# Zero products ahead of the first head mix, and the first batch's v loaded by pairs of heads, twice

## The chip, the cores and the metric

The kernel runs on one core of a Trainium2 chip. The metric is the device time of one launch in microseconds; three runs give a median of 743.95 (743.8 to 744.45). Engines are called by the names of the profile: PE (matrix products), PEld (its weight loads), DVE (vector), ACT (scalar), POOL (GpSimd) and SP, whose queue issues every DMA of this kernel.

## The reference, cut to what matters

```python
scores = scale * np.matmul(q, k.transpose(0, 1, 3, 2))      # 2 batches, 12 heads, 448 rows, head size 64
scores = np.einsum('bhij,hg->bgij', scores, w_pre)          # first mix, over heads
scores = scores - np.max(scores, axis=-1, keepdims=True)
attn = np.exp(scores)
attn = attn / (np.sum(attn, axis=-1, keepdims=True) + 1e-09)
attn = np.einsum('bhij,hg->bgij', attn, w_post)             # second mix
x = np.matmul(attn, v)                                      # then as 896 x 768
# two feed-forward layers, 768 -> 2048 -> 768, first with ELU, then with SiLU
```

## The kernel before

The kernel computes attention first (to about 270 us of the trace) and the two layers after it. Attention works on eight tiles: batch 0 or 1, times four groups of up to 120 query rows. The scores of a tile lie in SBUF as rows by heads (`s`). A mix over heads needs heads on the partitions, so a DMA (`relayout`) brings ten query rows by twelve heads into a block of 120 partitions by 448 keys (`blk`, five buffers). There are twelve blocks in a full tile and nine in the fourth one, 90 in all.

An order written out by hand runs over the blocks: one call of `step(s)` issues the work of step s for each engine. In step s PE mixes block s (`premix`, `pre`), DVE takes the row maximum (`rmax`, `nmx`), ACT takes exp with the row sum (`exps`), and DVE makes the reciprocal of the sum for block s-1 (`recip`: `sum`, `kr`). PE makes the second mix of block s-2 (`postmix`, `post`), and ACT and DVE split the result of block s-3 into two fp16 parts (`post_hi`, `post_lo`, tile `a`). Other work hangs on the steps in tables: `QK_AT` (score products of the next tile, `pq`, and transposes of q, `ptq`), `KT_AT` (transposes of the second batch's k), `X_AT` (products with v, `av`), `P_AT` and `V_AT` (work on v), and `D_AT` (DMAs). Each engine runs its instructions in the order in which they are issued, and SP its DMAs too: a DMA that waits holds all behind it.

v is used as two fp16 parts after a scaling by a power of two, so its largest magnitude must be known first. `v_max` takes the maximum of two heads at a time (DVE), and `v_scale` brings the six results to one scale in three stages: a DVE reduction, a PE transpose with a DVE reduction (`vpa`, `vmb`), and a PE broadcast (`vpb`) followed by six small DVE instructions. `prep_v` makes the parts of a pair: two ACT instructions, and the remainders either on DVE (even pairs of batch 0, `v_lo` in the next step) or on POOL (`vf`, then a subtraction).

For batch 0, all of v comes in step 0 by three DMAs of 448 KB (`vraw`), ahead of the relayout of block 5. The maxima stand in steps 1 to 6, the scale in 7 to 9, the parts in 9 to 12. The first products with v stand in step 15, two heads in every second step from then on. Batch 1's v comes by pairs (`vr`, two buffers, 224 KB each): the loads for the maxima in steps 16 to 26, the maxima in 18 to 28, the scale in 30 to 32, and a second load for the parts from step 39 on.

Ahead of step 0 the first tile is built under a PSUM pool of its own. PE runs 14 products on zeros, then transposes of q and k, then six pairs of score products. A pair's two heads fill one PSUM tile of two banks, from which ACT takes the first head and DVE the second. Relayouts 0 to 4 follow, then the transposes of the second tile's q, and then step 0.

Of the kernel before, what the change touches and what calls it, by code (L numbers as in the profile page):

```python
# [8 lines left out]
F32 = mybir.dt.float32  # L9
# [4 lines left out]
AF = mybir.ActivationFunctionType  # L14
ALU = mybir.AluOpType
AX = mybir.AxisListType
PSUM = bass.MemoryType.PSUM

P = 128
B, H, S, D = 2, 12, 448, 64  # L20
# [3 lines left out]
NP = H // 2  # L24
CP = S // 4
# [6 lines left out]
NBLK = 5  # L32
PREB = 3
NWARM = 14
NE = 3
LAG = (2, 3)

# [2 lines left out]
def attn_moe_moe(ctx: ExitStack, tc: tile.TileContext, q, k, v, w_pre, w_post, w1i, w1o, w2i, w2o, out):  # L40
    nc = tc.nc
# [9 lines left out]
    cm_b, bp = pool("attn1", bufs=1, side="right")  # L51
    cm_a, ap_ = pool("attn2", bufs=1, side="left")
    cm_p0, p0 = pool("ps0", bufs=1, space=PSUM)
    psp = [p0]
# [100 lines left out]
    def transpose_q(T, g):  # L155
        m = prows(tiles[T][1])
        raw = raws["q", T]
        pt = ps.tile([P, S], F32, name=f"ptq{T}_{g}", tag="pre", bufs=PREB) if T else p0.tile([P, S], F32, name=f"ptq{T}_{g}", tag="t", bufs=3)
        pt = pt[:, :3 * TI]
        pt = pt.rearrange("p (j c) -> p j c", j=3)  # L160
        for j in range(3):
            p = 3 * g + j
            nc.tensor.transpose(pt[:, j, :m], raw[:m, 2 * p:2 * p + 2].rearrange("p e d -> p (e d)"), ident[:m, :m])
        if g == 0:
            qT[T] = wp.tile([P, 2, NP, P], F32R, name=f"qt{T}", tag="qT", bufs=3)
        t = qT[T][:, :, 3 * g:3 * g + 3, :m]

        o = [t[:, i].rearrange("p j (r n) -> p j r n", r=BI) for i in range(2)]
        tev.append((o[0], o[1], pt[:, :, :m].rearrange("p j (n r) -> p j r n", r=BI)))

    def transpose_hi():

        for hi, lo, src in tev:
            nc.scalar.copy(hi, src)
# [10 lines left out]
    ones = cp.tile([1, P], F32, name="ones1")  # L185
    nc.vector.memset(ones, 1.0)

    def load_v0(g):
        if g == 0:
            vraw[0] = ap_.tile([CP, H, 4, D], F32, name="vraw0", tag="a", bufs=2)  # L190
        nc.sync.dma_start(vraw[0][:, 4 * g:4 * g + 4], v[0, 4 * g:4 * g + 4].rearrange("h (p r) d -> p h r d", r=4))

    def load_v1(p):
        raw = bp.tile([CP, 2, 4, D], F32, name=f"vr_{p}", tag="vr", bufs=2)
        nc.sync.dma_start(raw, v[1, 2 * p:2 * p + 2].rearrange("h (p r) d -> p h r d", r=4))
        vraw[1, p % NP] = raw

    def v_max(b, p):
        if p == 0:
            vmx[b] = cp.tile([CP, NP], F32, name=f"vmx{b}")  # L200
        raw = vraw[0][:, 2 * p:2 * p + 2] if b == 0 else vraw[1, p]
        nc.vector.tensor_reduce(vmx[b][:, p:p + 1], raw.rearrange("p h r d -> p (h r d)"), axis=AX.X, op=ALU.max, apply_absolute_value=True)

    vst = {}

# [30 lines left out]
    def prep_v(b, p):  # L236

        t = ap_.tile([CP, 4, 2, P], F16, name=f"v16_{b}_{p}", tag="v16", bufs=7)
        sc = vs[b][0][:CP]
        raw = vraw[0][:, 2 * p:2 * p + 2] if b == 0 else vraw[1, p]  # L240
        for e in range(2):
            hi = t[:, :, e, e * D:(e + 1) * D]
            nc.scalar.activation(hi, raw[:, e], AF.Copy, scale=sc)
            lo = t[:, :, e, (1 - e) * D:(2 - e) * D]
            if b or p % 2:
                full = ap_.tile([CP, 4, D], F32, name=f"vf{p}_{e}", tag="vf", bufs=2)
                nc.gpsimd.tensor_scalar(full, raw[:, e], sc, None, op0=ALU.mult)
                nc.gpsimd.tensor_tensor(lo, full, hi, op=ALU.subtract)
            else:
                vev.append((lo, raw[:, e], sc, hi))  # L250
        v16[b, p] = t
# [5 lines left out]
    def qk_pair(T, p):  # L257

        b, t = tiles[T]
        m = prows(t)  # L260
        if T not in smap:
            smap[T] = bp.tile([TI, H, S], F32, name=f"s{T}", tag="s", bufs=2)
        qt, kt = qT[T][:, :, p], kT[b, p]
        pq = psp[0].tile([P, 2, 512], F32, name=f"pq{T}_{p}", tag="mm", bufs=2 if T == 0 else 1)[:m, :, :S]
        for n, (i, j) in enumerate(((0, 0), (0, 1), (1, 0))):
            for e in range(2):
                half = slice(e * D, (e + 1) * D)
                nc.tensor.matmul(pq[:, e], qt[half, i, :m], kt[half, j, :], start=(n == 0), stop=(n == 2))  # L268
        sev.append((T, p, m, pq))

    def qk_evac():
        for T, p, m, pq in sev:
            o = smap[T][:m, 2 * p:2 * p + 2, :]
            if T == 0:
                nc.scalar.activation(o[:, 0], pq[:, 0], AF.Copy, scale=0.125)
                nc.vector.tensor_scalar(o[:, 1], pq[:, 1], 0.125, None, op0=ALU.mult)
            else:
                nc.scalar.activation(o, pq, AF.Copy, scale=0.125)
        sev.clear()
# [14 lines left out]
    def relayout(n):  # L294

        T, i0, ni = blocks[n]
        t = bp.tile([TI, S], F32, name=f"blk{n}", tag="blk", bufs=NBLK)
        k = nblk(tiles[T][1])
        i = i0 // BI
        dl[n] = nc.sync.dma_start(t[:ni * H], smap[T][i:i + k * (ni - 1) + 1:k])  # L300
        blk[n] = t
# [150 lines left out]
    cm_p0.__exit__(None, None, None)  # L452
    cm_ps, ps = pool("psA", bufs=1, space=PSUM)
    psp[0] = ps
    transpose_q(1, 0)
    transpose_q(1, 1)
    transpose_hi()
    transpose_lo()
    prep_mix()
# [2 lines left out]

    NB = len(blocks)
    NT_ = len(tiles)
    QK_AT, KT_AT, X_AT, P_AT, V_AT, D_AT = {}, {}, {}, {}, {}, {}

    def at(d, step, f):
        d.setdefault(int(step), []).append(f)

    for T in range(NT_):  # L470
        b, t = tiles[T]
        f, l = first[T], last[T]
        sc = (l - f + 1) / 12
        if T + 1 < NT_:
            nb, nt_ = tiles[T + 1]
            for p in range(NP):
                st = (max(2 * p - 2, p if p < 2 else 0) if T == 0 else int(f + (2 * p - 2) * sc + 8) - 8)
                at(QK_AT, st, lambda TT=T + 1, p=p: qk_pair(TT, p))
                if nt_ == 3 and nb + 1 < B:
                    at(KT_AT, st + 3, lambda p=p, bb=nb + 1: transpose_k(bb, p))  # L480
                    at(D_AT, st - 3 if p < 2 else st, lambda p=p, bb=nb + 1: load_k(bb, p))
            n0 = NBLK if T + 1 == 0 else 0
            for n in range(first[T + 1] + n0, last[T + 1] + 1):
                at(D_AT, max(l - 1, n - NBLK + 1), lambda n=n: relayout(n))
        if T + 2 < NT_:
            at(D_AT, 0 if T == 0 else f + 1, lambda TT=T + 2: load_q(TT))
            for g in range(2):
                at(QK_AT, l - 3 + 2 * g, lambda TT=T + 2, g=g: transpose_q(TT, g))
        for p in range(NP):
            if T + 1 < NT_:  # L490
                nsc = (last[T + 1] - l) / 12
                st = l + 1 + LAG[1] + (p if T + 2 == NT_ else int(2 * p * nsc))
            for h in (2 * p, 2 * p + 1) if T + 1 < NT_ else ():
                at(X_AT, st, lambda T=T, h=h: av_head(T, h))
            if t == 3 and b + 1 < B:
                v1 = [l - 1] + [l + 2 + LAG[1] + int(2 * j * nsc) for j in range(NP - 1)]
                at(V_AT, v1[p], lambda p=p, b=b: prep_v(b + 1, p))
                at(D_AT, l - 5 + p if p < 2 else v1[p - 2] + 2, lambda p=p: load_v1(p))
    for n in range(NBLK, last[0] + 1):
        at(D_AT, n - NBLK + 1, lambda n=n: relayout(n))  # L500
    for g in range(3):
        at(D_AT, 0, lambda g=g: load_v0(g))
    for p in range(NP):
        at(V_AT, 1 + p, lambda p=p: v_max(0, p))
        at(V_AT, 9 + 0.7 * p, lambda p=p: prep_v(0, p))
        at(D_AT, 16 + 2 * p, lambda p=p: load_v1(p))
        at(V_AT, 18 + 2 * p, lambda p=p: v_max(1, p))
    for b, st in ((0, 7), (1, 30)):
        for i in range(3):
            at(V_AT if i == 0 else P_AT, st + i, lambda b=b, i=i: v_scale(b, i))  # L510

    def run(d, s):
        for f in d.get(s, []):
            f()

    def step(s):
        def do(f, n):
            if 0 <= n < NB:
                f(n)

        do(premix, s)
        run(QK_AT, s)
        run(P_AT, s)
        do(post_hi, s - LAG[1])
        do(rmax, s)
        do(recip, s - 1)
        do(post_lo, s - LAG[1])
        v_lo()
        av_sum()
        av_swap()  # L530
        av_evac()
        run(X_AT, s)
        run(KT_AT, s)
        do(postmix, s - LAG[0])
        do(exps, s)
        transpose_hi()
        qk_evac()
        transpose_lo()
        run(V_AT, s)
        run(D_AT, s)  # L540


# [409 lines left out]
```

## Time and profile before

| | before |
|---|---|
| median of 3 runs | 743.95 us |
| the profiled execution: time / span | 746.99 us / 745.2 us |
| PE busy in the span | 722.4 us, 97% |
| DVE / ACT / POOL busy | 516.2 / 398.1 / 74.7 us |
| granted PE clock, mean | 0.991 |

A line of a timeline gives start, duration, engine, line of the kernel, operation, output and inputs, shapes and count, and in brackets how long the engine was idle before it and what ended that. A PE instruction on fp32 counts twice (x2 is one product of the first mix), and its end is modelled, so costs on PE are read from one start to the next.

### The profile page before, as it was taken

The page shows a single profiled execution, that of the slowest core. Times are in us where ns is not written, and L with a number is a line of the kernel's source. Part 1 is how long each engine was busy: PE and PEld are TensorE (multiplying, and loading weights), DVE is VectorE, ACT ScalarE, POOL GpSimd, SP SyncE. Part 2 cuts the span into 40 slices and gives each one's busy share as a digit, 9 for nine tenths or more (in the row PEclk, how much of TensorE's full clock was granted, in tenths as well). Part 3 has the DMA queues.
Part 4 walks back from the last instruction along what each step waited for, and adds up shares of the span by engine and source line. Part 5 has one row for each costly group of instructions (what it writes and reads, how often), then busy time and mean ns, then how long its engine had stood idle before and what let it go on. Part 6 is the DMA issues. An engine that isn't in the chain of part 4 may idle for free.

```text
span 745.2 us, 12122 instructions
## 1 busy us (share of the span) xinstructions
PE 722.4 (97%) x4472; PEld 616.4 (83%) x4472; DVE 516.2 (69%) x1147; ACT 398.1 (53%) x789; POOL 74.7 (10%) x99
## 2 busy tenths in 40 slices
PE   7889999999998899999999999999999999999998
PEld 4456766776775688999999999999999999999997
DVE  5687877677776868888885556567888888833800
ACT  5577767788775657666663223335555555312301
POOL 1033011355123320000000000000000000000000
PEclk9899999999999999999999999999999999999999
DMA  6724735344325233333333333342333334633402
GB/s 121 219 82 130 188 103 146 117 122 142 105 95 173 81 114 106 105 109 107 106 102 104 113 113 113 113 127 83 110 104 108 106 107 119 183 102 106 139 1 74
DMA packets 90435, 85.70 MB, mean 115 GB/s; under 512 B 32664, under 2 KB 86280, under 8 KB 90376
## 3 DMA queue, kind: packets, MB, share of 16 engines
q1 hardware_dynamic: 90376, 84.93, 39.0%
q8 instruction: 35, 0.57, 0.3%
q14 instruction: 24, 0.20, 0.1%
HBM read 60.05 MB, written 2.75 MB: 84 GB/s over the span
## 4 chain that ended last, share of the span: by engine, by line
PE 90%; DVE 5%; DMA 3%; SPq 1%; ACT 1%; issue 0%; ACTq 0%
PE ph L716 30%; PE po L769 16%; PE post L352 9%; PE pre L310 7%; PE py L791 5%; PE py L789 5%; PE py L790 5%; PE pq L268 4%; PE av L385 4%; PE ph_mm L716 1%; DVE a L366 1%; DVE nmx L318 1%; DMA vraw<-in_v_dram 1%; DMA xs<-xt 1%; DVE kr L341 1%; PE ptk L151 1%
## 5 line engine op out<-in xcount | busy, mean ns | idle before, releaser
L716 PE MATMUL ph<-x,we 128*128 128x448 f32 x1116 | 231.0, 369 | 2.5 <-ACT x L559 1.5
L716 PEld LDWEIGHTS ph<-x,we 128*128 128x128 f32 x1116 | 210.7, 189 | 22.2 <-ACT x L559 1.8
L352 PE MATMUL post<-kr,pe 120*112 120x120 f32 x720 | 93.8, 273 | 9.0 <-DVE a L366 8.5
L769 PE MATMUL po<-g,we 128*128 128x448 f32 x468 | 101.5, 366 | 0.0
L352 PEld LDWEIGHTS post<-kr,pe 120*112 120x112 f32 x720 | 80.5, 177 | 25.1 <-issue 17.7
L769 PEld LDWEIGHTS po<-g,we 128*128 128x128 f32 x468 | 87.8, 188 | 7.9
L328 ACT ACTIVATE pe<-pre,nmx 120x448 f32<-120x448 f32 x90 | 57.1, 634 | 62.9 <-DVE sum L338 54.2
L310 PE MATMUL pre<-blk,kpre 120*120 120x448 f32 x180 | 85.3, 556 | 2.4 <-DMA blk<-s 2.4
L318 DVE TENSOR_REDUCE nmx<-pre 120x1 f32<-120x448 f32 x90 | 55.9, 622 | 43.9 <-PE pre L310 43.6
L617 ACT ACTIVATE wr<-wr 128x384 f32<-128x384 f32 x126 | 67.3, 545 | 35.5 <-DMA wr<-in_moe_w_out_dram 31.2
L652 ACT CAST we<-wc 128x768 fp32r<-128x768 f32 (+1 forms) x63 | 51.0, 809 | 41.8 <-PE py L791 22.3
L659 DVE TENSOR_TENSOR we<-wc,we 128x768 fp32r<-128x768 f32 (+1 forms) x63 | 58.6, 930 | 19.5 <-ACT we L652 16.7
L632 DVE SCALAR_TENSOR_TENSOR wc<-wr,wc 128x384 int32<-128x384 int32 x126 | 68.8, 546 | 4.3
L634 DVE SCALAR_TENSOR_TENSOR wc<-wr,wc 128x384 int32<-128x384 int32 x126 | 68.5, 543 | 3.3
L366 DVE TENSOR_TENSOR a<-post,a 112x480 f16<-112x480 f32 x90 | 58.5, 650 | 5.2 <-ACT a L361 5.2
L790 PE MATMUL py<-we,g 128*128 128x384 f32 x182 | 61.0, 335 | 0.0
L791 PE MATMUL py<-we,g 128*128 128x384 f32 x182 | 61.0, 335 | 0.0
L789 PE MATMUL py<-we,g 128*128 128x384 f32 x182 | 61.0, 335 | 0.0
L385 PEld LDWEIGHTS <-v 112*128 112x128 f16 x768 | 42.2, 99 | 20.5 <-issue 18.3
L361 ACT ACTIVATE a<-post 112x480 f16<-112x480 f32 x90 | 51.6, 573 | 6.5 <-PE post L352 6.5
L385 PE MATMUL av<-a,v 112*128 112x120 f16 (+1 forms) x768 | 46.0, 215 | 0.9 <-DVE a L366 0.9
L268 PEld LDWEIGHTS pq<-kt,qt 64*120 64x120 f32 (+1 forms) x288 | 21.9, 175 | 29.2 <-ACT a L361 11.2
(111 smaller groups left out, 866.6 us busy)
## 6 DMA issues: line engine op xcount, KB each, us to landing
wr<-in_moe_w_in_dram SPq DMA_DIRECT2D x58, 384.0 KB
wr<-in_moe_w_out_dram SPq DMA_DIRECT2D x56, 384.0 KB
blk<-s SPq DMA_DIRECT2D x90, 210.0 KB
wr<-in_moe_w_out_dram SPq DMA_DIRECT2D x12, 256.0 KB
vr<-in_v_dram SPq DMA_DIRECT2D x12, 224.0 KB
out_dram<-y SPq DMA_DIRECT2D x14, 192.0 KB
early<-in_moe_w_in_dram SPq DMA_DIRECT2D x6, 384.0 KB
xs<-xt SPq DMA_DIRECT2D x36, 60.0 KB
```

Source lines behind the costliest of these rows:

```text
L310: nc.tensor.matmul(t[:r], kpre[:r].rearrange("p i h -> p (i h)")[:, :r], blk.pop(n)[:r], start=True, stop=True)
L352: nc.tensor.matmul(t[:CP, j, :, :ni], pp[:r, j * CP:(j + 1) * CP], k[:r, :, :ni], start=True, stop=True)
L366: nc.vector.tensor_tensor(a[:, 1, :, :, i0:i0 + ni], pst.pop(n)[:CP, :, :, :ni], a[:, 0, :, :, i0:i0 + ni], op=ALU.subtract)
L385: nc.tensor.matmul(o, vt[:, j, h % 2, :], a[:, c, j, h, :m], start=(c == 0 and j == 0), stop=(c == 1 and j == 3))
L617: nc.scalar.activation(hf, hf, AF.Copy, scale=2.0 ** -112)
L632: nc.vector.scalar_tensor_tensor(cc, r[:, :, 1], -2147483648, cc, op0=ALU.bitwise_and, op1=ALU.bitwise_or)
L634: nc.vector.scalar_tensor_tensor(cc, r[:, :, 0], 29, cc, op0=ALU.logical_shift_right, op1=ALU.bitwise_or)
L716: nc.tensor.matmul(ph, wt[:, kk * P:(kk + 1) * P], xq[hf, kk][:, xi], start=(n_ == 0), stop=(n_ + 1 == len(terms)))
L769: nc.tensor.matmul(po, wt[:, kk * P:(kk + 1) * P], g_out1(k0 + kk, gi, hf), start=(k0 == 0 and n_ == 0), stop=(k0 + kn == KF and n_ == 3 * ...
L789: nc.tensor.matmul(py, gh, hi[:, w_], start=(kf == 0), stop=False)
L790: nc.tensor.matmul(py, gh, lo[:, w_], start=False, stop=False)
L791: nc.tensor.matmul(py, gl, hi[:, w_], start=False, stop=(kf == KF - 1))
```

## The change

- Sixteen products on zeros are issued on PE ahead of step 0: seven before the transposes of the second tile's q and nine after them. They write a buffer of the `pre` ring that nothing reads.
- In the first tile, a pair's score products go to two PSUM tiles of one bank each, in place of one tile of two banks.
- v of batch 0 is loaded by pairs, as that of batch 1 is, through the same two buffers, and twice. The loads for the maxima stand in steps 0, 0, 2, 4, 6 and 8, those for the parts in steps 10, 12, ... 20. The maxima stand in steps 2, 4, 6, 8, 9 and 10, the scale in 10 to 12, and the parts in steps 13, 15, ... 23.
- Batch 1's first loads move to steps 24 to 34, its maxima to 26 to 36 and its scale to 38 to 40.
- The PE stages of the scale (`P_AT`) are issued after `exps` in a step, no longer right after the first mix.
- Relayouts have a table of their own (`R_AT`), issued ahead of a step's other DMAs.

```diff
+NKEEP = (7, 9)
...
-    def load_v0(g):
-        if g == 0:
-            vraw[0] = ap_.tile([CP, H, 4, D], F32, name="vraw0", tag="a", bufs=2)
-        nc.sync.dma_start(vraw[0][:, 4 * g:4 * g + 4], v[0, 4 * g:4 * g + 4].rearrange("h (p r) d -> p h r d", r=4))
-    def load_v1(p):
-        raw = bp.tile([CP, 2, 4, D], F32, name=f"vr_{p}", tag="vr", bufs=2)
-        nc.sync.dma_start(raw, v[1, 2 * p:2 * p + 2].rearrange("h (p r) d -> p h r d", r=4))
-        vraw[1, p % NP] = raw
+    def load_v(b, p):
+        raw = bp.tile([CP, 2, 4, D], F32, name=f"vr{b}_{p}", tag="vr", bufs=2)
+        nc.sync.dma_start(raw, v[b, 2 * p:2 * p + 2].rearrange("h (p r) d -> p h r d", r=4))
+        vraw[b, p] = raw
...
-        pq = psp[0].tile([P, 2, 512], F32, name=f"pq{T}_{p}", tag="mm", bufs=2 if T == 0 else 1)[:m, :, :S]
+        if T == 0:
+            pq = [p0.tile([P, S], F32, name=f"pq0_{p}_{e}", tag=f"mm{e}", bufs=2)[:m] for e in range(2)]
+        else:
+            pq = psp[0].tile([P, 2, 512], F32, name=f"pq{T}_{p}", tag="mm", bufs=1)[:m, :, :S]
...
+    def keep(i):
+        t = ps.tile([P, S], F32, name=f"keep{i}", tag="pre", bufs=PREB)
+        for _ in range(NKEEP[i]):
+            nc.tensor.matmul(t, wz[:, :P], wz, start=True, stop=True)
+
+    keep(0)
     transpose_q(1, 0)
     transpose_q(1, 1)
+    keep(1)
...
-                at(D_AT, max(l - 1, n - NBLK + 1), lambda n=n: relayout(n))
+                at(R_AT, max(l - 1, n - NBLK + 1), lambda n=n: relayout(n))
...
-        at(D_AT, n - NBLK + 1, lambda n=n: relayout(n))
-    for g in range(3):
-        at(D_AT, 0, lambda g=g: load_v0(g))
+        at(R_AT, n - NBLK + 1, lambda n=n: relayout(n))
     for p in range(NP):
-        at(V_AT, 1 + p, lambda p=p: v_max(0, p))
-        at(V_AT, 9 + 0.7 * p, lambda p=p: prep_v(0, p))
-        at(D_AT, 16 + 2 * p, lambda p=p: load_v1(p))
-        at(V_AT, 18 + 2 * p, lambda p=p: v_max(1, p))
-    for b, st in ((0, 7), (1, 30)):
+        at(D_AT, max(0, 2 * p - 2), lambda p=p: load_v(0, p))
+        at(V_AT, (2, 4, 6, 8, 9, 10)[p], lambda p=p: v_max(0, p))
+        at(D_AT, 10 + 2 * p, lambda p=p: load_v(0, p))
+        at(V_AT, 13 + 2 * p, lambda p=p: prep_v(0, p))
+        at(D_AT, 24 + 2 * p, lambda p=p: load_v(1, p))
+        at(V_AT, 26 + 2 * p, lambda p=p: v_max(1, p))
+    for b, st in ((0, 10), (1, 38)):
         for i in range(3):
             at(V_AT if i == 0 else P_AT, st + i, lambda b=b, i=i: v_scale(b, i))
...
         do(premix, s)
         run(QK_AT, s)
-        run(P_AT, s)
...
         do(exps, s)
+        run(P_AT, s)
         transpose_hi()
         qk_evac()
         transpose_lo()
         run(V_AT, s)
+        run(R_AT, s)
         run(D_AT, s)
```

## Rows read from the trace of the kernel before

**Rows 1.** Windows: stretch, length, busy time of each engine, PE clock, DMA share, GB/s.
```profile
18.20:19.87 1.67, 0.00 (x1) 0.04 (x1) 1.48 (x9) 0.00 (x0) 0.00 (x0) 0.52 0.58 220
19.87:25.00 5.13, 5.13 (x12) 1.91 (x14) 0.90 (x3) 1.64 (x3) 0.00 (x0) 0.50 0.86 222
...
60.43:108.00 47.57, 47.57 (x406) 33.98 (x405) 37.02 (x104) 33.53 (x73) 5.76 (x9) 1.00 0.61 165
```

**Rows 2.** Timeline of PE, from before step 0 to step 15.
```profile
16.69 0.81 PE L163 MATMUL ptq<-ident,q 120*128 120x120 f32 x6 [1.04 <-DMA q<-in_q_dram]
19.87 1.82 PE L310 MATMUL pre<-blk,kpre 120*120 120x448 f32 x2 [2.37 <-DMA blk<-s]
...
41.96 0.53 PE L163 MATMUL ptq<-ident,q 120*128 120x120 f32 x3
...
60.43 0.92 PE L310 MATMUL pre<-blk,kpre 120*120 120x448 f32 x2
```

**Rows 3.** The chain that ended last, 14 to 32 us: start, length, what.
```profile
15.70 0.55 ACT s L275
...
16.27 0.64 DVE s L276
...
16.93 0.85 SPq L300
...
21.68 6.72 DMA vraw<-in_v_dram
```

**Rows 4.** Waits from 19.8 to 60.43 us: total, times, longest.
```profile
PE post L352 <- DVE a L366: 3.6, 6, 1.6
```

**Rows 5.** Timeline of DVE in steps 6 and 7.
```profile
37.52 0.61 DVE L318 TENSOR_REDUCE nmx<-pre 120x1 f32<-120x448 f32 x1
...
39.78 0.61 DVE L318 TENSOR_REDUCE nmx<-pre 120x1 f32<-120x448 f32 x1
...
41.46 0.15 DVE L210 TENSOR_REDUCE vma<-vmx 112x1 f32<-112x6 f32 x1
```

**Rows 6.** Instructions of line 276: what ended its engine's idle time (us, times).
```profile
  ACT s L275: 1.5, 6
```

**Rows 7.** Timeline of PE's weight loads for zero products at the start.
```profile
4.66 0.29 PEld L434 LDWEIGHTS <-wz 128*128 128x128 f16 x2 [0.20 <-issue]
4.85 0.29 PEld L434 LDWEIGHTS <-wz 128*128 128x128 f16 x2
```

**Rows 8.** Timeline of PE in steps without a wait.
```profile
62.89 0.92 PE L310 MATMUL pre<-blk,kpre 120*120 120x448 f32 x2
...
64.54 1.07 PE L352 MATMUL post<-kr,pe 120*112 120x120 f32 x8
65.45 0.92 PE L310 MATMUL pre<-blk,kpre 120*120 120x448 f32 x2
...
123.85 0.92 PE L310 MATMUL pre<-blk,kpre 120*120 120x448 f32 x2
...
125.42 0.92 PE L310 MATMUL pre<-blk,kpre 120*120 120x448 f32 x2
```

**Rows 9.** Timeline of ACT: exp, a score pair's read, and parts of v.
```profile
22.38 0.63 ACT L328 ACTIVATE pe<-pre,nmx 120x448 f32<-120x448 f32 x1 [4.34 <-DVE nmx L318]
...
23.14 0.92 ACT L278 ACTIVATE s<-pq 120x896 f32<-120x896 f32 x1
...
53.03 1.70 ACT L243 ACTIVATE v<-vraw,sc_v 112x256 f16<-112x256 f32 x4
```

**Rows 10.** Timeline around the scale of batch 1, step 32.
```profile
107.43 0.16 DVE L220 COPY vmc<-vpb 128x1 f32<-128x1 f32 x1 [1.71 <-PE vpb L218]
...
110.98 0.60 PE L151 MATMUL ptk<-ident,kr 112*128 112x112 f32 x4 [0.98 <-ACT s L278]
```

**Rows 11.** POOL's instructions for parts of v: duration ns min/median/max.
```profile
L248 POOL TENSOR_TENSOR v<-vf,v x18: 667/672/805, 48.7 to 178.6; 112x256 f16<-112x256 f32 x18
L247 POOL TENSOR_SCALAR vf<-vraw,sc_v x6: 922/922/1096, 46.1 to 58.1; 112x256 f32<-112x256 f32 x6
```

More of the change, by code (lines that the diff above doesn't have):

```diff
@@ L200, in v_max @@
             vmx[b] = cp.tile([CP, NP], F32, name=f"vmx{b}")
-        raw = vraw[0][:, 2 * p:2 * p + 2] if b == 0 else vraw[1, p]
-        nc.vector.tensor_reduce(vmx[b][:, p:p + 1], raw.rearrange("p h r d -> p (h r d)"), axis=AX.X, op=ALU.max, apply_absolute_value=True)
+        nc.vector.tensor_reduce(vmx[b][:, p:p + 1], vraw[b, p].rearrange("p h r d -> p (h r d)"), axis=AX.X, op=ALU.max, apply_absolute_value=True)
     vst = {}
@@ L239, in prep_v @@
         sc = vs[b][0][:CP]
-        raw = vraw[0][:, 2 * p:2 * p + 2] if b == 0 else vraw[1, p]
+        raw = vraw[b, p]
         for e in range(2):
@@ L267, in qk_pair @@
                 half = slice(e * D, (e + 1) * D)
-                nc.tensor.matmul(pq[:, e], qt[half, i, :m], kt[half, j, :], start=(n == 0), stop=(n == 2))
+                nc.tensor.matmul(pq[e] if T == 0 else pq[:, e], qt[half, i, :m], kt[half, j, :], start=(n == 0), stop=(n == 2))
         sev.append((T, p, m, pq))
@@ L274, in qk_evac @@
             if T == 0:
-                nc.scalar.activation(o[:, 0], pq[:, 0], AF.Copy, scale=0.125)
-                nc.vector.tensor_scalar(o[:, 1], pq[:, 1], 0.125, None, op0=ALU.mult)
+                nc.scalar.activation(o[:, 0], pq[0], AF.Copy, scale=0.125)
+                nc.vector.tensor_scalar(o[:, 1], pq[1], 0.125, None, op0=ALU.mult)
             else:
@@ L464, in attn_moe_moe @@
     NT_ = len(tiles)
-    QK_AT, KT_AT, X_AT, P_AT, V_AT, D_AT = {}, {}, {}, {}, {}, {}
+    QK_AT, KT_AT, X_AT, P_AT, V_AT, R_AT, D_AT = {}, {}, {}, {}, {}, {}, {}
     def at(d, step, f):
@@ L497, in attn_moe_moe @@
                 at(V_AT, v1[p], lambda p=p, b=b: prep_v(b + 1, p))
-                at(D_AT, l - 5 + p if p < 2 else v1[p - 2] + 2, lambda p=p: load_v1(p))
+                at(D_AT, l - 5 + p if p < 2 else v1[p - 2] + 2, lambda p=p: load_v(1, p))
     for n in range(NBLK, last[0] + 1):
-        at(D_AT, n - NBLK + 1, lambda n=n: relayout(n))
-    for g in range(3):
-        at(D_AT, 0, lambda g=g: load_v0(g))
+        at(R_AT, n - NBLK + 1, lambda n=n: relayout(n))
     for p in range(NP):
-        at(V_AT, 1 + p, lambda p=p: v_max(0, p))
-        at(V_AT, 9 + 0.7 * p, lambda p=p: prep_v(0, p))
-        at(D_AT, 16 + 2 * p, lambda p=p: load_v1(p))
-        at(V_AT, 18 + 2 * p, lambda p=p: v_max(1, p))
-    for b, st in ((0, 7), (1, 30)):
+        at(D_AT, max(0, 2 * p - 2), lambda p=p: load_v(0, p))
[5 more added lines that the diff above has]
+    for b, st in ((0, 10), (1, 38)):
         for i in range(3):
```

## The prediction

> **What bounds the kernel now.** I first ask where PE, 97% busy, is not the bound, since only there can a rearrangement move the end. The windows [rows 1] answer it: from 60.43 to 108 us PE is busy for all 47.57 us. What starts earlier at 60.43 is earlier at the end, and what is added behind 60.43 on DVE, ACT, POOL or the DMAs is free as long as PE finds its data. So the question is when step 15, the first with a product with v, begins. The timeline of PE [rows 2] puts step 0 at 19.87 and step 15 at 60.43: 40.56 us for fifteen steps. There the reader is to see a wait of 2.37 us for the first block ahead of step 0, and before it 1.04 us for q. The clock is the next thing to see [rows 1]: after these two waits it has fallen to its lower level, 1.2 GHz (a mean of 0.52 up to 19.87), and all of 19.87 to 25.00 runs at 0.50.
>
> The chain that ended last [rows 3] names what holds the first steps beside the clock. DVE's last read of scores starts at 16.27; the relayouts issue one after another on SP from 16.93; v's first DMA issues behind them at 21.68 and lands 6.72 us later. Until then DVE, which has the first maximum of v in step 1, can't go on to the row maxima behind it. From there the timeline of DVE [rows 5] shows steps of 2.26 us (37.52 to 39.78) with a maximum of v and 1.68 us without one, with no idle time inside: DVE paces steps 3 to 7. The waits of PE [rows 4] add 3.6 us in six waits for DVE's second fp16 part, the longest 1.6 us, in the steps where v's parts are made.
>
> **The parts of the change.** I build the new time of step 15 from its new start and from the shortest steps that PE shows.
>
> *Start of step 0.* In the first tile DVE reads the second head's bank only when ACT has read the first head's: ACT ended DVE's idle time in all six cases, 1.5 us in total [rows 6]. For the last pair ACT starts at 15.70 and DVE at 16.27 [rows 3]. With a tile for each head, DVE can start with ACT, 0.57 us earlier, and the relayouts with it: the first block lands at about 19.32 and not 19.87. Bounds: nothing, if DVE waits for something else, up to 0.57. I take 0.55.
>
> The Trainium skill, page "PSUM — Partial Sum Buffer", section "Specifications (TRN2)", says that ACT and DVE can read PSUM in parallel at full bandwidth while they are in different banks. The two heads are in different banks, yet the trace shows the wait of 1.5 us in six cases. By the rule the wait is an order that the shared tile imposes and goes with the split, for 0.55 us; by the row alone it could be in the reads, and the split would bring nothing.
>
> The zero products cost 0.19 us each at the full clock (4.66 to 4.85 [rows 7], which also shows that products on zeros alone reached that level). PE ends the last scores at about 15.68; seven products are 1.33 us, to 17.01; the six transposes of q are 0.81 us [rows 2], to 17.82; nine products are 1.71 us, to 19.53. So PE, not the DMA, starts step 0, at 19.53: 0.34 us gained. At half the clock sixteen products would be 6.1 us, the transposes about 1.6, and step 0 would start at 23.4, 3.5 us late.
>
> *The clock.* With PE busy to 19.53 I take the full clock in steps 0 to 2. The 5.13 us at 0.50 [rows 1] then shrink to half: 2.57 us. Bounds: nothing to 2.57 us.
>
> *Steps 0 to 14 on PE.* The shortest steps come from starts without a wait [rows 8]. First mix, scores, second mix: 62.89 to 65.45, 2.56 us. First and second mix only: 123.85 to 125.42, 1.57 us. First mix and scores: 62.89 to 64.54, 1.65 us. Steps 0 and 1 have no second mix: 3.30. Steps 2, 4, 6, 12 and 14 are of the long kind: 12.80. Steps 8 and 10 have three transposes of q more, at most 0.53 each [rows 2]: 6.18. Steps 3, 5, 7, 9, 11 and 13 are short: 9.42. The two small products of the scale are bounded by 0.53 each; I take 0.6 for both. The sum is 32.3 us.
>
> To this come waits that stay. In step 1 the scores need the one `mm` buffer, which ACT empties after a row maximum (0.61 [rows 5]), an exp (0.63) and the read (0.92 [rows 9]), 2.2 us with hops from the first mix's end; PE has 1.65 us to do. I take 0.75 us there and 0.25 in step 2, together 1.0.
>
> *DVE beside it.* For steps 3 to 14 DVE needs 12 x 1.68 = 20.2 us, five maxima at 0.58 (2.26 less 1.68) = 2.9, and for two remainders of q, two of v and eight small instructions at most 4 x 0.61 + 8 x 0.15 = 3.6: 26.7 us. PE's sum for the same steps is 32.3 - 3.3 - 2.6 = 26.4. The two are level, so each hands the other small waits; the maxima lie mostly in long steps (2.26 against 2.56 us), but those of steps 9 and 10 don't fit. I take 0.8 us, from nothing to 1.8.
>
> *The first load of v.* The load now is half the size. At the 222 GB/s of that stretch [rows 1], 224 KB less are 1.0 us, so instead of 6.72 us after 21.68 it lands 5.7 us after 21.13, at 26.8, and the maximum in step 2 ends at 27.4. PE reaches the end of step 3's first mix at 19.53 + 3.30 + 1.0 + 2.56 + 0.76 = 27.15. DVE is 0.25 us late there and has 0.3 us to spare in step 4: nothing. If it landed as before, 1.0 us later, some 0.7 would be left.
>
> So step 15 begins at 19.53 + 32.3 + 1.0 + 0.8 = 53.6, 6.8 us earlier than 60.43.
>
> *v's parts in steps 13 to 23.* ACT gets two instructions in each second step, 1.70 / 2 = 0.85 us [rows 9], in a step in which it has an exp and one fp16 part: about 2 us, below the 2.46 that PE has there. Their cover is PE's work; without it they would cost 6 x 0.85 = 5.1 us. DVE's remainders come in step 14, 18 and 22 at the end of the step, and the product with v follows right behind the next first mix: I take 0.5 us in step 15 and 0.1 later, 0.6 in all.
>
> *The second loads* put six DMAs of some 0.5 us of issue and 1 us of transfer on SP and the DMA engines. Each waits for the parts two pairs back, and behind it stand relayouts and the swaps; a relayout is issued four steps, about 10 us, ahead of its first mix. Nothing. *The maxima of batch 1* go from steps 18 to 28 to steps 26 to 36, where k's transposes give DVE work too, but in the odd steps: 2.26 us against 2.56. Nothing.
>
> *The scale after exp.* In step 32 of before, DVE waited 1.71 us for the scale's broadcast with that step's row maximum queued behind it; ACT came late, and PE waited 0.98 us [rows 10]. Now this stands at the end of a step. I take 0.7 of the 0.98 (nothing to 1.0).
>
> The sum: 6.8 - 0.6 + 0.7 = 6.9 us. The profiled execution would go from 746.99 to 740.1 (span 745.2 to 738.3). The median of the runs is 3.0 us below that execution, so I take the gain from it: 743.95 - 6.9 = **737.05**.
>
> **The rivals.**
>
> *The clock falls all the same.* PE has gaps of 0.75 and 0.25 us in steps 1 and 2. For it: before, it fell after 1.04 and part of 2.37 us of waiting. Against: it stayed up through the wait of 1.6 us [rows 4] later on. Price up to 2.57 us: 739.6.
>
> *v's parts come late.* In odd pairs POOL has four instructions in order, 2 x (0.92 + 0.67) = 3.2 us [rows 11], after ACT's parts, and two steps are 5.0 us, of which a good half is left. If each of the six pairs held PE by 0.5 us, the gain would be 3.0 us smaller: 740.0.
>
> *The change doesn't do what it says at the start*: the split leaves the order of the reads as it is. Step 0 starts at 19.87 and 0.34 us are lost: 737.4, within the forecast's own range.
>
> *It becomes slower.* SP is one queue, and the loads of pairs 2 to 5 wait on it for the maxima two pairs back, with relayouts behind them. Pairs 0, 2 and 4 form a chain: load, maximum in step 2, load, maximum in step 6, load, maximum in step 9. Steps 2 to 6 are 8.3 us and 6 to 9 are 5.7 on PE's sum. With the 6.72 us of the first load, taken when the queue was full, the first link fits and the second is about 1.6 us late. Counting 0.7 us for a maximum, the two links lose the 6.9 us from about 9.8 us a load on (2 x 10.5 - 14.0). At 12 us the lateness is 4.4 + 7.0 = 11.4 us: 748.5. Against it: after the first blocks a load finds the queue nearly empty.
>
> *Nothing changes:* an unseen wait eats it all; no row speaks for it.
>
> **How the numbers follow.** The forecast, with the split's failure, from 735.1 (no coupling, DMA-bound start, 1.0 us at step 32) to 738.6: 0.66. The clock: 0.12. v's parts late: 0.10. Nothing: 0.05. Slower: 0.05. A smaller mixture of losses between 738.6 and 742.4: 0.02. The range 735.1 to 740.6 takes in the first three, less a few of their tails. A measurement of this kernel can tell some 0.2%, 1.5 us, from no change: faster 0.90, same 0.05, slower 0.05.
>
> **What would show it.** PE's timeline: no wait ahead of step 0, first mix of step 0 near 19.5 and 0.85 us to the scores behind it; clock 1.00 through 25 us; the first maximum of v ending near 27.4; step 15 near 53.6; the 0.98 us wait near 111 gone. DVE's second read in the first tile starts with PE's end and not with ACT's. I would be wrong if PE waits for blocks in steps 6 to 10, if waits for v appear in steps 15 to 25, or if waits between DVE and PE in steps 3 to 14 add up to more than 2 us.

## The result and the profile after

Four runs of the changed kernel have a median of 736.3 us (732.63 to 738.16), beside 743.88 us for the kernel before on the same chip. The ratio is 0.9885, with a 95% interval of 0.9852 to 0.9918: 1.15% faster, some 8.6 us. The profiled execution took 735.47 us with a span of 733.8 us, against 746.99 and 745.2.

The first windows show the clock, which stood at 0.50 from 19.87 to 25.00 us before [rows 1]. The columns are the same.

```profile
15.00:18.00 3.00, 2.84 (x19) 1.83 (x20) 1.26 (x3) 1.19 (x4) 0.00 (x0) 1.00 0.18 26
18.00:19.50 1.50, 1.50 (x9) 0.59 (x7) 1.34 (x4) 0.42 (x2) 0.00 (x0) 1.00 0.62 235
19.50:22.00 2.50, 2.50 (x11) 1.04 (x10) 1.43 (x6) 0.76 (x3) 0.00 (x0) 1.00 0.66 242
22.00:25.00 3.00, 2.40 (x11) 1.03 (x12) 1.46 (x5) 2.41 (x4) 0.00 (x0) 1.00 1.07 198
```

From 15.16 us on PE works without a gap up to step 0, on zeros for most of the time, and the clock stays at its upper level, 2.4 GHz. The timeline of PE gives the same points as [rows 2] and the waits between them:

```profile
15.76 1.50 PE L458 MATMUL keep<-wz 128*128 128x448 f16 x7
...
17.71 1.87 PE L458 MATMUL keep<-wz 128*128 128x448 f16 x9
19.56 0.98 PE L309 MATMUL pre<-blk,kpre 120*120 120x448 f32 x2
20.47 0.87 PE L267 MATMUL pq<-kt,qt 64*120 64x448 f32 x6
...
22.82 0.87 PE L267 MATMUL pq<-kt,qt 64*120 64x448 f32 x6 [0.54 <-ACT s L277]
...
45.73 0.26 PE L209 MATMUL vpa<-ident,vma 112*1 112x112 f32 x1 [0.34 <-DVE vma L206]
...
53.10 0.92 PE L309 MATMUL pre<-blk,kpre 120*120 120x448 f32 x2
53.90 1.00 PE L384 MATMUL av<-a,v 112*128 112x120 f16 x16
```

Step 0 starts at 19.56 and step 15 at 53.10, where they stood at 19.87 and 60.43. Between them PE has two waits, 0.54 and 0.34 us; the first product with v follows the first mix of step 15 with no wait. On DVE, the first pair of v is there at 26.90 and costs 1.03 us of idle time, and the row maxima go on right behind it:

```profile
26.90 0.69 DVE L198 TENSOR_REDUCE vmx<-vr 112x1 f32<-112x512 f32 x1 [1.03 <-DMA vr<-in_v_dram]
27.50 0.61 DVE L317 TENSOR_REDUCE nmx<-pre 120x1 f32<-120x448 f32 x1
...
29.18 0.61 DVE L317 TENSOR_REDUCE nmx<-pre 120x1 f32<-120x448 f32 x1
```

I followed the first mix of every step through both timelines. The lead over the kernel before grows to 2.44 us at step 3, 4.92 at step 10 and 7.33 at step 15. It holds to within 0.1 us up to step 32, becomes 9.10 at step 34 (before's wait of 0.98 us [rows 10] is gone) and 8.49 at step 42, where the scale of batch 1 now stands. There it stays to step 78 (8.44). Behind it the two traces differ by 2.9 us more, to 11.4 at the end, in a part of the kernel that wasn't changed. First the lead grows to 11.2 us by step 89, the last: in the trace of before, PE waits 3.02 us at step 80, as ACT stands 3.90 us (for a DMA, by the profile) ahead of its first work on the layers' weights (`early`); in the changed kernel PE waits 0.74 us there.

```profile
230.62 0.54 ACT L617 ACTIVATE early<-early 128x384 f32<-128x384 f32 x1 [3.90 <-DMA blk<-s]
...
232.46 1.10 PE L352 MATMUL post<-kr,pe 120*112 120x120 f32 x8 [3.02 <-DVE a L366]
```

```profile
221.74 1.04 PE L351 MATMUL post<-kr,pe 120*112 120x120 f32 x8 [0.74 <-DVE a L365]
```

Behind step 89 the changed kernel's trace loses 2.1 us at a wait for the last x and gains 2.3 us by PE's pace; both come up with E8, E10 and E11. The long wait at step 80 stands in two of the fourteen traces, before's and E12's (3.49 us), and is 0.51 to 1.28 us in the others. Those two kernels have neither the zero products nor v's new order, but whether that shortens the wait no run shows.

### The profile page after: what moved, and what is told of

It reads as the page before. It is cut to its first block, busy times and chain, and to the rows that moved or that the text cites. A ratio compares the mean times of both kernels' runs of the same rounds, so it can differ in the third digit from the quotient of the medians.

```text
span 733.8 us, 12170 instructions
## 1 busy us (share of the span) xinstructions
PE 719.2 (98%) x4488; PEld 617.4 (84%) x4488; DVE 514.4 (70%) x1147; ACT 397.8 (54%) x789; POOL 73.5 (10%) x99
## 4 chain that ended last, share of the span: by engine, by line
PE 93%; DVE 4%; DMA 2%; ACT 1%; issue 0%; ACTq 0%
PE ph L724 31%; PE po L777 16%; PE post L351 10%; PE pre L309 8%; PE py L799 5%; PE py L798 5%; PE py L797 5%; PE pq L267 5%; PE av L384 4%; DMA xs<-xt 1%; PE ph_mm L724 1%; DVE nmx L317 1%; PE warm L433 1%; DVE a L365 1%; PE ptk L152 1%; PE ptq L164 1%
## 5 line engine op out<-in xcount | busy, mean ns | idle before, releaser
L309 PE MATMUL pre<-blk,kpre 120*120 120x448 f32 x180 | 83.1, 543 | 0.0
```

The costliest lines, as they stand in the source:

```text
L309: nc.tensor.matmul(t[:r], kpre[:r].rearrange("p i h -> p (i h)")[:, :r], blk.pop(n)[:r], start=True, stop=True)
```

## The experiments

The table gives for each run the ratio to the kernel before with its interval, and from its one trace the start of steps 15, 34 and 42, counted from the start of step 0. Step 0 itself lay between 19.43 and 20.17 us in the fourteen traces. In four traces of the changed order (the first one, E8, E10, E11) step 15 lies at 33.54 us each time and step 42 within 0.03 us, so differences of a tenth can be read here, while the ratios have intervals of 0.5 to 1.3%.

| | ratio | step 15 | step 34 | step 42 |
|---|---|---|---|---|
| before | 1 | 40.56 | 92.37 | 114.17 |
| changed | 0.9885 (0.9852 to 0.9918) | 33.54 | 83.58 | 105.99 |
| E1 no zero products | 0.9897 (0.9834 to 0.9961) | 35.70 | 85.91 | 108.32 |
| E2 one score tile | 0.9880 (0.9827 to 0.9934) | 33.53 | 83.59 | 105.99 |
| E3 v as before | 0.9930 (0.9904 to 0.9956) | 40.65 | 91.53 | 113.32 |
| E4 zero products alone | 0.9971 (0.9944 to 0.9998) | 41.53 | 93.35 | 115.15 |
| E5 maxima early | 0.9899 (0.9852 to 0.9945) | 35.25 | 85.28 | 107.67 |
| E6 parts one step later | 1.0152 (1.0100 to 1.0204) | 33.53 | 101.51 | 123.91 |
| E7 scale early in the step | 0.9884 (0.9848 to 0.9920) | 35.40 | 85.39 | 107.89 |
| E8 zero products in the tail | 0.9860 (0.9819 to 0.9901) | 33.54 | 83.58 | 105.99 |
| E9 order of v alone | 0.9915 (0.9883 to 0.9947) | 37.50 | 87.54 | 110.03 |
| E10 changed, again | 0.9885 (0.9862 to 0.9909) | 33.54 | 83.58 | 105.98 |
| E11 zero products in the tail, again | 0.9819 (0.9795 to 0.9842) | 33.54 | 83.62 | 106.01 |
| E12 scale late alone | 0.9985 (0.9949 to 1.0021) | 39.61 | 90.49 | 112.29 |

**E1, the changed kernel without the zero products.**

```diff
-    keep(0)
     transpose_q(1, 0)
     transpose_q(1, 1)
-    keep(1)
```

> The changed kernel without its sixteen zero products. Step 0 and step 15 start at 19.56 and 53.10 us in the changed kernel. If the products earn their place by the clock, it falls to 1.2 GHz during the wait for the first block, step 0 starts near 19.3 and runs at half the clock, and step 15 comes up to 2.4 us later, near 55.5. If the slow clock is hidden behind v's first load (DVE is held by it to 27.4 us anyway), the loss is at most 1 us and step 15 stands near 54.

Its windows:

```profile
18.00:19.50 1.50, 0.01 (x1) 0.04 (x1) 1.40 (x6) 0.13 (x1) 0.00 (x0) 0.50 0.64 245
19.50:22.00 2.50, 2.50 (x6) 1.14 (x8) 1.16 (x5) 0.00 (x0) 0.00 (x0) 0.50 0.65 237
22.00:25.00 3.00, 3.00 (x10) 1.12 (x10) 0.47 (x1) 1.64 (x3) 0.00 (x0) 0.53 1.11 204
```

The clock falls in the idle stretch as before, and step 15 comes 2.16 us later from step 0 (35.70 against 33.54). The zero products are worth that, given the new order of v; their gain is not hidden behind v's load.

**E2, one tile of two banks for a pair's scores.**

```diff
-        if T == 0:
-            pq = [p0.tile([P, S], F32, name=f"pq0_{p}_{e}", tag=f"mm{e}", bufs=2)[:m] for e in range(2)]
-        else:
-            pq = psp[0].tile([P, 2, 512], F32, name=f"pq{T}_{p}", tag="mm", bufs=1)[:m, :, :S]
+        pq = psp[0].tile([P, 2, 512], F32, name=f"pq{T}_{p}", tag="mm", bufs=2 if T == 0 else 1)[:m, :, :S]
```

> The changed kernel with one PSUM tile of two banks for a pair's scores in the first tile, as before. If the split took the wait of DVE for ACT away, DVE's last read starts 0.55 us later here, the first block lands near 19.87, and step 0 starts there, 0.3 us later than 19.56: step 15 near 53.4. If the order of the reads has another cause, nothing changes and step 15 stays at 53.1.

What ended DVE's idle time ahead of its reads, as in [rows 6], and its last read in E2's timeline:

```profile
  ACT s L271: 1.5, 6
```

```profile
16.41 0.62 DVE L272 TENSOR_SCALAR s<-pq 120x448 f32<-120x448 f32 x1 [0.53 <-ACT s L271]
```

In the changed kernel's timeline the same read waits for PE, and starts beside ACT's:

```profile
15.86 0.54 ACT L274 ACTIVATE s<-pq 120x448 f32<-120x448 f32 x1 [0.61 <-PE pq L267]
15.90 0.62 DVE L275 TENSOR_SCALAR s<-pq 120x448 f32<-120x448 f32 x1 [0.26 <-PE pq L267]
```

So the wait of 1.5 us belongs to the shared tile: it is there in six of six reads with it and gone without it. Step 0 stands at 20.00 us here, and between 19.44 and 20.03 in the four traces of the changed order, as the work ahead of it starts earlier or later from trace to trace. Counted from the first zero product (15.72 here, 15.76 in the changed kernel), the split shows: step 0 comes 4.28 us after it in E2 and 3.78 to 3.97 in those four, and PE waits ahead of it in E2 and not in the changed kernel:

```profile
20.00 0.98 PE L306 MATMUL pre<-blk,kpre 120*120 120x448 f32 x2 [0.45 <-DVE sc_w L92]
```

The profile names DVE's `sc_w`, but in the changed kernel step 0 starts ahead of that one (19.56 against 19.88); what is late in E2 is the first relayout, issued at 17.06 and not at 16.61. E4, with zero products and the shared tile, has the same 0.45 us and 4.27. So the split is worth 0.3 to 0.5 us at step 0; behind it nothing differs.

**E3, the changed kernel with v as before.**

```diff
+    for g in range(3):
+        at(D_AT, 0, lambda g=g: load_v0(g))
     for p in range(NP):
+        at(V_AT, 1 + p, lambda p=p: v_max(0, p))
+        at(V_AT, 9 + 0.7 * p, lambda p=p: prep_v(0, p))
+        at(D_AT, 16 + 2 * p, lambda p=p: load_v1(p))
+        at(V_AT, 18 + 2 * p, lambda p=p: v_max(1, p))
-        at(D_AT, max(0, 2 * p - 2), lambda p=p: load_v(0, p))
-        at(V_AT, (2, 4, 6, 8, 9, 10)[p], lambda p=p: v_max(0, p))
-        at(D_AT, 10 + 2 * p, lambda p=p: load_v(0, p))
-        at(V_AT, 13 + 2 * p, lambda p=p: prep_v(0, p))
-        at(D_AT, 24 + 2 * p, lambda p=p: load_v(1, p))
-        at(V_AT, 26 + 2 * p, lambda p=p: v_max(1, p))
-    for b, st in ((0, 10), (1, 38)):
+    for b, st in ((0, 7), (1, 30)):
```

> The changed kernel with v as in the kernel before (one tile for batch 0 loaded at once, maxima in steps 1 to 6, scale in 7 to 9, parts in 9 to 12, batch 1 in 16 to 32); zero products, split scores, and the order of relayouts and scale stages stay changed. If v's order was what held steps 1 to 14, DVE waits for v to about 27.9, the steps with a maximum take 2.26 us again and the parts cost some 3.6 us: step 15 near 58 to 59.5, about 5 us later than 53.1. If start and clock carried the gain, step 15 stays near 55.

Two lines of its waits up to 62 us, and a window:

```profile
PE post L356 <- DVE a L370: 3.0, 3, 1.6
PE post L356 <- DVE kr L345: 2.1, 1, 2.1
```

```profile
28.00:32.00 4.00, 2.69 (x10) 1.71 (x10) 3.86 (x12) 3.07 (x7) 0.00 (x0) 0.71 0.70 237
```

Step 15 is at 40.65, where the kernel before has it: the whole gain of the first fifteen steps is gone, though start, zero products and split are in place. The start is won and then lost again: PE waits 2.1 us for DVE, which waits for v, and now the clock falls there (0.71). I had expected step 15 about 5 us later than in the changed kernel; it is 7.1 us later. E3 undoes loads, maxima, scale steps and parts together. Of these only the maxima are undone by themselves (E5); the parts were not.

**E4, the kernel before with the zero products alone.**

```diff
+    keep(0)
     transpose_q(1, 0)
     transpose_q(1, 1)
+    keep(1)
```

> The kernel before with the sixteen zero products added and nothing else. If the clock's cost in steps 0 to 2 was on the path, step 15 comes 2 to 2.6 us earlier than 60.43, near 58. If DVE's wait for v's first load (28.4 us) hides it, the first steps run at the full clock and step 15 stays within 0.5 us of 60.43.

A DVE and a PE line of its timeline, and a window:

```profile
28.72 0.69 DVE L203 TENSOR_REDUCE vmx<-vraw 112x1 f32<-112x512 f32 x1 [4.58 <-DMA vraw<-in_v_dram]
...
30.57 1.94 PE L353 MATMUL post<-kr,pe 120*112 120x120 f32 x8 [2.61 <-DVE kr L342]
```

```profile
28.00:32.00 4.00, 1.43 (x7) 1.43 (x8) 3.14 (x10) 2.02 (x5) 0.00 (x0) 0.79 0.82 251
```

I had two outcomes in mind, a gain of about 2 us and none. Neither came: step 15 is 0.97 us later than before. v lands when it lands; the faster steps only make DVE wait longer for it (4.58 us, not 2.31), PE stands for 2.61 us, and the clock falls behind that wait in place of the first. Its runs are 0.3% shorter than before's all the same, with an interval that just leaves out 1; as step 42 comes later, that lies in a part of the kernel that wasn't changed. In the traces it is step 80: PE waits 0.54 us there in E4 and 3.02 in before, and from 1.28 us behind at step 78 E4 comes to 1.88 us ahead at step 89.

**E5, the maxima back in steps 1 to 6**, with four buffers so that the loads can stand ahead of them.

```diff
-        raw = bp.tile([CP, 2, 4, D], F32, name=f"vr{b}_{p}", tag="vr", bufs=2)
+        raw = bp.tile([CP, 2, 4, D], F32, name=f"vr{b}_{p}", tag="vr", bufs=4)
...
-        at(D_AT, max(0, 2 * p - 2), lambda p=p: load_v(0, p))
-        at(V_AT, (2, 4, 6, 8, 9, 10)[p], lambda p=p: v_max(0, p))
+        at(D_AT, max(0, p - 3), lambda p=p: load_v(0, p))
+        at(V_AT, 1 + p, lambda p=p: v_max(0, p))
```

> The changed kernel with the maxima of batch 0's v back in steps 1 to 6 (four buffers for v's pairs, so that loads stand in steps 0, 0, 0, 0, 1 and 2); loads by pairs, scale and parts stay changed. If the place of the maxima matters, DVE stands in step 1 for v's first pair until 26.9 us and the row maximum of step 2 behind it, so that step 3 and all later steps come 1 to 2.5 us later: step 15 at 54.1 to 55.6. If only the size of the loads and the place of the parts matter, step 15 stays within 0.5 us of 53.1.

```profile
27.25 0.69 DVE L198 TENSOR_REDUCE vmx<-vr 112x1 f32<-112x512 f32 x1 [3.26 <-DMA vr<-in_v_dram]
```

```profile
29.10 1.07 PE L351 MATMUL post<-kr,pe 120*112 120x120 f32 x8 [1.29 <-DVE kr L340]
```

These are a DVE and a PE line of E5's timelines. Step 15 is 1.71 us later. One step earlier, the first maximum has the row maximum of step 2 behind it, and DVE waits 3.26 us where it waited 1.03. So of the order of v, the place of the maxima is worth 1.7 us.

**E6, the parts one step ahead of use instead of two.**

```diff
-        at(V_AT, 13 + 2 * p, lambda p=p: prep_v(0, p))
+        at(V_AT, 14 + 2 * p, lambda p=p: prep_v(0, p))
```

> The changed kernel with the parts of batch 0's v in steps 14, 16, ... 24, one step ahead of use in place of two. Step 15 to 27 then shows how much room the two steps leave. If the parts are ready well ahead of use, nothing changes. By the rows, POOL needs 3.2 us for an odd pair and one step is 2.5 us, of which PE comes to the product with v after 0.8: each odd pair holds PE 1.5 to 2.5 us, each even pair up to 1.7 us, and step 27 comes 6 to 12 us later than the 84.0 of the changed kernel.

Two products with v in PE's timeline, the lines of the waits that name v, and one window:

```profile
56.45 1.00 PE L384 MATMUL av<-a,v 112*128 112x120 f16 x16 [2.34 <-DVE v L228]
...
62.62 0.59 PE L384 MATMUL av<-a,v 112*128 112x120 f16 x8 [1.00 <-POOL v L244]
```

```profile
PE av L384 <- DVE v L228: 7.3, 4, 2.3
PE av L384 <- POOL v L244: 5.7, 6, 1.1
```

```profile
70.00:80.00 10.00, 7.59 (x53) 4.83 (x53) 5.37 (x15) 5.00 (x13) 3.73 (x5) 0.83 0.29 80
```

Six pairs one step later cost 17.9 us (101.51 against 83.58 at step 34; the same at step 27) and make the kernel 1.5% slower than the one before. 13.0 us are waits for v; the clock falls behind some of them (0.83 on average from 70 to 80 us), which my 6 to 12 us had left out. It is at 0.50 from 72.85 to 76.2 and from 89.95 to 93.3 us, so up to 3.4 of the other 4.9 us can be its fall.

**E7, the scale's PE stages right behind the scores again.**

```diff
         run(QK_AT, s)
+        run(P_AT, s)
         do(post_hi, s - LAG[1])
...
         do(exps, s)
-        run(P_AT, s)
```

> The changed kernel with the PE stages of the scale right behind the first mix and the scores, as before. If their place in the step made the difference at step 32, the wait now stands in steps 39 and 40: step 42, at 125.55 us in the changed kernel, comes about 1 us later, and steps 11 and 12 cost up to 1 us more as well. If that difference only came from the steps that were chosen (30 to 32 had transposes of k beside the scale), nothing changes.

In PE's timeline of steps 11 to 14:

```profile
45.65 0.26 PE L209 MATMUL vpa<-ident,vma 112*1 112x112 f32 x1 [1.28 <-DVE vma L206]
...
51.42 0.84 PE L351 MATMUL post<-kr,pe 120*112 120x120 f32 x6 [1.08 <-DVE a L365]
```

Step 15 comes 1.86 us later, twice what I expected, and from there to step 42 it takes 72.49 us against 72.45. For batch 0 the place in the step is worth 1.86 us. The last maximum stands at the end of step 10, and the transpose at the start of step 11 has to wait for it: step 11 is 0.8 us longer. Step 13, where PE waits 1.08 us for DVE's second fp16 part, is 1.2 us longer. For batch 1, in steps 38 to 40, it is worth nothing.

**E9, the order of v alone on the kernel before** (E1, E2 and E7 together, and the relayouts in the old table).

```diff
-    keep(0)
...
-    keep(1)
...
-        at(R_AT, n - NBLK + 1, lambda n=n: relayout(n))
+        at(D_AT, n - NBLK + 1, lambda n=n: relayout(n))
...
+        run(P_AT, s)
...
-        run(P_AT, s)
```

> The kernel before with the new order of v alone: loads by pairs and twice, maxima, scale and parts in the new steps; no zero products, one score tile, the scale's PE stages early in the step, relayouts in the old table. If the parts add up as the runs with one part undone say (2.1 us for the zero products, 0.4 for the split, 1.8 for the place of the scale's stages), step 15 stands near 53.1 + 4.3 = 57.4. If they overlap, it stands nearer to 55.2, where the run without zero products had it; if the new order needs them all, it stands near 60.

Step 15 lies at 37.50, 3.06 us ahead of before and 3.96 behind the changed kernel. The zero products (2.16, E1) and the place of the scale's stages (1.86, E7) make 4.02. Taken from the changed kernel the parts add up, which leaves next to nothing, counted from step 0, for the relayouts' own table; that was not undone alone. Put on the kernel before, one by one, they don't: -0.97 (E4), 0.95 (E12) and 3.06 us make 3.0, of 7.02 in all.

**E12, the kernel before with the scale's stages late in the step.**

```diff
-        run(P_AT, s)
         do(post_hi, s - LAG[1])
...
         do(exps, s)
+        run(P_AT, s)
```

> The kernel before with the scale's PE stages behind exp in a step and nothing else. Steps 8, 9, 31 and 32 have them. If their place caused the wait of 0.98 us behind step 32, step 34 comes about 1 us earlier relative to step 30 (12.79 us in the trace of before, 10.97 in that of the changed kernel), 11.6 to 11.8. If the steps chosen caused it, the 12.79 us stay. Steps 8 to 11 may gain up to 1 us as well.

Step 30 to step 34 takes 11.86 us, 0.93 less than before, and step 15 comes 0.95 earlier. So the wait of 0.98 us did come from the place in the step; but E7 shows that the new steps avoid it as well: with the old place its steps 30 to 34 take 10.97 us, as in the changed kernel. Either edit would have done against that wait.

**E8, E10 and E11: the part behind step 78.** In the first layer PE waits for the last x, 3.21 us in the changed kernel's first trace, and runs at half the clock behind it. E8 and E11 fill the wait with fourteen more zero products, in a PSUM buffer that was free.

```diff
+NTAIL = 14
...
     moe_in(2, 0, 2, 0)
+    kt = ps.tile([P, S], F32, name="keept", tag="post", bufs=2)
+    for _ in range(NTAIL):
+        nc.tensor.matmul(kt, wz[:, :P], wz, start=True, stop=True)
```

> The changed kernel with fourteen more zero products after PE's last work ahead of the first layer's second part, where PE waits some 2 to 3 us for the last x. If the clock's fall there costs time, these 2.7 us of zero products keep it at 1.00, the next 5.4 us don't run at 0.50, and the time falls by 2 to 2.7 us from the changed kernel's; the spread of its runs shrinks. If the x behind the wait is late by itself (the engines that make it set the pace), the clock stays up and the time is the same within 0.5 us.

> The changed kernel again, beside the next run. Step 15 and step 42 stand as in its first trace (33.5 and 106.0 us after step 0) if the gain up to there is fixed by the order of the work. What varies between its runs must then lie behind step 78: the waits at steps 79 to 81 and ahead of the first layer's second part, the clock there, and PE's own pace in the two layers (107.3 or 105.7 us, 234.5 or 236.8 us in the traces so far).

> The changed kernel with fourteen zero products in PE's wait for the last x, again, beside the changed kernel on the same chip. If the half clock behind that wait costs the changed kernel 2 to 2.7 us in most of its runs, the median here is 1 to 2.7 us lower. If PE's pace in the layers decides, the two medians are within 1 us.

PE's timeline around the wait and a window behind it, first of the changed kernel (E10), then with the products (E11):

```profile
263.38 3.95 PE L724 MATMUL ph<-x,we 128*128 128x448 f32 x18
269.19 0.47 PE L724 MATMUL ph<-x,we 128*128 128x448 f32 x1 [1.86 <-ACT x L567]
```

```profile
272.00:274.00 2.00, 2.00 (x7) 1.78 (x6) 1.97 (x4) 1.60 (x4) 0.00 (x0) 0.50 0.50 147
```

```profile
266.19 2.82 PE L845 MATMUL keept<-wz 128*128 128x448 f16 x14
268.76 0.47 PE L725 MATMUL ph<-x,we 128*128 128x448 f32 x1
```

```profile
272.00:274.00 2.00, 2.00 (x12) 1.85 (x11) 1.97 (x5) 1.63 (x4) 0.00 (x0) 1.00 0.67 203
```

The products keep the clock: twelve instructions on PE in 2 us at 1.00 where there were seven at 0.50. The mean clock is 1.00 in all eleven runs of E8 and E11, and 0.995 to 0.998 in the six of E10. On one chip E11's median is 732.69 us (732.25 to 734.95, 5 runs) beside 737.72 for E10 (737.18 to 739.89, 6 runs) and 747.16 for the kernel before, a ratio of 0.9819. That beats both kernels, and by more than the 1 to 2.7 us that I had expected. E8, the same kernel on another chip, has a ratio of 0.9860 (median 734.77 us), which can't be told from the changed kernel's 0.9885, and its runs spread over 6.1 us, where I had expected less than the changed kernel's 5.5.

Not all of the 5.0 us is the clock. PE has two paces in the layers, in stretches in which it never waits and the clock is 1.00. The products with the first weights of a layer (`ph`) come in two groups, one for each layer. The second group up to 520 us, in E10 and in E11 (count, duration in ns as min/median/max, first and last start):

```profile
L724 PE MATMUL ph<-x,we x113: 368/368/369, 496.8 to 519.9; 128*128 128x448 f32 x113
```

```profile
L725 PE MATMUL ph<-x,we x130: 362/365/369, 493.7 to 519.8; 128*128 128x448 f32 x130
```

From one start to the next that is 207 and 203 ns, 2% apart. The first group, here E10's, has the faster pace in every trace but E8's:

```profile
L724 PE MATMUL ph<-x,we x490: 362/365/369, 279.8 to 378.9; 128*128 128x448 f32 x164
```

The slower pace of the second group costs a trace 2.3 us (236.8 us or 234.5 from the first product with the second weights of the first layer, `po`, to the same of the second layer, `py`). Before, E1, E4, E5, E6, E8 and E10 have it; the changed kernel's first trace, E2, E3, E7, E9, E11 and E12 don't. What sets it stays open.

The traces of E10 and E11 are 5.4 us apart (737.67 and 732.25 us). Of these 0.9 lie ahead of step 89, 2.2 between step 89 and the 51st product of the first group, with the wait and the half clock, and 2.3 are the pace. So the zero products account for 2.2 us of E11's lead in these two traces. E8's trace reaches that product 1.5 us sooner after step 89 than E10's, though it runs at the slower pace from its first group on.

## Why the prediction was right

The time lies in the range, 0.75 us below the value given. The parts, in the order of the prediction:

*The start of step 0*, 0.34 us, came out at 0.31 (19.53 predicted, 19.56 measured), with PE and not the DMA starting it. The step behind it, that the split takes DVE's wait away, is shown by E2, and without the split PE would have waited 0.45 us longer there. The Trainium skill, page "PSUM — Partial Sum Buffer", section "Specifications (TRN2)", lets ACT and DVE read different banks in parallel; the trace agrees, as the two heads are read at the same time once they are in tiles of their own (15.86 and 15.90 us). But 0.31 against 0.34 is luck in part: step 0 lay between 19.44 and 20.03 us in four traces of the changed order.

*The clock*, 2.57 us, measured 2.16 (E1). I had named no condition for it, and E4 shows that there is one: without v's new order it is worth -0.97 us, as the wait, and the fall of the clock with it, move behind the first load. The rival that the clock falls all the same did not come true in the changed kernel, which passed the gap of step 1 at 1.00. Where v is late, in E3 and E4, the clock does fall, but at another place than I put it: behind the wait for v's load (0.71 and 0.79).

*The first load of v* was to land at 26.8; the maximum started at 26.90.

*The steps* were the mis-sized term, on the safe side. I had 32.3 us of work, 1.0 of waits and 0.8 of coupling between DVE and PE, 34.1; measured were 33.54. Steps 0 to 2 came out as summed (6.87 us). Of the coupling nothing shows: steps 3 to 7 take the shortest times that I had for them, and so does step 9, a short one with a maximum in it. Steps 8 and 10 are 0.5 us shorter than I had them, as the three transposes of q cost less than the bound. Steps 11 to 13 are 0.7 us longer, with the wait of 0.34 us for the scale in them. So the total is nearer than its terms. E5 prices the place of the maxima: 1.7 us if they stand one step earlier.

*v's parts* were to cost 0.6 us in steps 15 to 23; they cost 0.05 (the lead goes from 7.33 to 7.28). As a rival I gave their lateness 3.0 us, from half a microsecond for each pair. E6 shows a sharper edge: one step less, and a pair holds PE by 2.3 us (DVE) or 2 x 1.0 us (POOL), with the clock's fall on top. The condition was right, the price six times too low, and the pairs that DVE finishes are held as well as POOL's.

*The scale after exp* was to give 0.7 of 0.98 us at step 32. The lead grows by 1.82 us there (7.28 to 9.10) and falls by 0.61 by step 42, 1.21 net. The place in the step gives 0.93 of it alone (E12), the new steps give all of it without the place (E7). That the place in the step would also be worth 1.86 us in steps 11 to 14 (E7), I hadn't seen: I wrote of it only for batch 1.

*The queue on SP*, the mechanism of the slower rival, was held by loads of v as described, and nobody waited: no wait for a block shows behind step 0.

Up to step 78 this makes 8.4 us, where I had 6.9; too little by 0.5 in the steps, 0.6 for v and 0.5 at the scale. The median fell by 7.6 and the ratio says 8.6. That the median came within 0.75 us of the value is in part luck: three terms were too small by 1.6 us in all, and the part behind step 78, on which the prediction has no term, could have moved it as far. The runs of the changed kernel spread over 5.5 us; in the traces the half clock in the tail (2.2 us) and the two paces (2.3 us) are about that much together, but the runs without a trace don't show which of them had which.

## What to carry to other kernels

A wait that several causes share is only gained when the last of them goes: zero products at the front were worth 2.2 us or minus 1.0 us, depending on whether a load further on was still late. So price an edit against what is late next, and try it both on the old and on the new kernel. Work that must be ready for another engine wants a lead counted in whole steps of the bound engine; one step less cost 17.9 us here, two were free. And where PE stands before a stretch of work that it bounds, products on zeros in a free PSUM buffer hold its clock, at the front as in the tail.

## What the runs showed of the hardware

PE's pace on the same products differs by 2% at a granted clock of 1.00 (207 and 203 ns from start to start, E10 and E11; 368 and 365 ns of duration in the median), over some 113 us without any wait on PE. In E10 it differs between the two layers of one execution; the cause is open.

Ahead of the last x PE's clock fell behind waits of 1.30 us (E4) to 3.21 us (the changed kernel's first trace; E10: 1.86 us, then 0.50), but not in E3, E7 and E12, whose waits were 1.95, 1.80 and 1.66 us. At step 80 it fell behind before's wait of 3.02 us (a mean of 0.57 from 233 to 237 us) and not behind E12's of 3.49 (1.00 from 230 to 237). So the length of the wait alone doesn't tell whether it costs the clock.
